# Y turned one step behind its gate, beside the sums of g, with the key search taken into the last attention steps (hgrn2 attention and a balanced expert layer)

## Chip, cores and metric

The kernel runs on one core of one Trainium2 chip. The metric is the device time of an execution in microseconds (us), lower is better. An execution that is profiled also leaves a trace, whose span is a little shorter than its own time.

## What is computed

First a recurrent attention: for each of 4 batches and 8 heads, over 768 positions with 48 dimensions, a 48x48 state is faded and added to. Then x, its output as 3072 tokens of 384, goes through a layer of 8 experts. Tokens are given to experts greedily, in the order of all logits, and each expert takes at most 384.

```python
f = 1 / (1 + np.exp(-f_logit))
for t in range(S):
    state = f[:, :, t, :, None] * state + einsum('bhd,bhe->bhde', k[:, :, t], v[:, :, t])
    y[:, :, t] = einsum('bhd,bhde->bhe', q[:, :, t], state)
x = y.transpose(0, 2, 1, 3).reshape(B * S, H * D)
logits = x @ w_gate                        # N x 8
for idx in argsort(-logits.flatten()):     # token, expert in falling order
    if assigned[tok] < 0 and counts[e] < N // E: assigned[tok] = e
for e in range(E):
    out[assigned == e] = relu(x[assigned == e] @ w1[e]) @ w2[e]
```

## The kernel before, in words

**Attention.** The 3072 positions are cut into 24 chunks of 128 (number i = 4c + b: chunk c of batch b). A chunk passes through some thirty small functions, its stages: `load_f`, `load_k`, `load_q`, `load_v` ask SP's queue for the inputs; `decays` (L166, L167, ScalarE) makes g, the logarithm of the decay; `cumulated` (L171, TensorE, bank L) sums g along the chunk; `clipped` (L176, VectorE) makes `dl` from it; `powers` and `scaled` (L187) make scaled q and k; `lengths` (L199) sums g over half chunks, `spanned` and `recorded` (L213, GpSimd) keep these; `turn_q`, `turn_k` (L232) transpose q and k on TensorE into the banks T[0] and T[1], and ScalarE copies them out (L240); `products` (L253) makes the new state's k-v products, except in the last four chunks; `scores` (L274) multiplies k and q into the banks A; `masked0`, `masked1` (L282, VectorE) copy them under a mask; `inner` (L304) and `outer` (L315) multiply them by v, and q by the old state, into the banks Y; `joined` adds the two Y banks (ScalarE copies one, L323, VectorE adds the other, L324) into `yT`; `gate` (L344) multiplies `yT` by the gate's weights, 16 small matmuls; `gated` copies the logits out; `turn_y` (L329) transposes `yT` by four matmuls into T[0], and `copy_y` (L334, ScalarE) takes it to `x`; `with_logits` (L351, GpSimd) adds the logits to the row, and `store` (L355) sends 128 rows to `xd` in memory through SP's queue.

**Order.** The order on every engine is written out by hand. A step runs all stages once, each for the chunk that its lag gives: the tuple `stages` (L358) lists stage and lag, so (`turn_y`, 3) works in step i + 3. Steps go from -1 to 25; steps 24 (`drain`, L365) and 25 (`finale`, L369) have lists of their own. `later(step, go, at)` hangs routing work into a step at the entry (None, at).

**Routing.** A token's key is its best logit, scaled by bounds on all logits (`bounds`, L505, in three parts at steps 20, 21, 22; it looks at the first four of six chunks of every batch) into `over`. `first_choices`, `overs`, `first_codes` prepare keys and choices. The search (`search`, L722) finds, for all experts at once, the key of the last token that still fits, in four digits of base 32. For each digit VectorE marks which keys are above each of 31 thresholds (`above`, L412), TensorE counts them by expert with 24 small matmuls (`cnt`, L735), VectorE takes `most` and `filled`, and one matmul adds the digit to `base` (L742). The first digit's marks and counts (`first_counts`, L545) are made during the drain and the finale. From `base` follow `code`, `kind` and each token's place (`positions`, L793), a sort by matmuls (`numbers`, L824; `sort`, L832, token matmuls L846) of the first expert's two token blocks (`found0`, `tok0`), whose rows GpSimd fetches by indirect DMA (`fetch`, L717); then the full sort, the token list, gathers of logits for tokens that are left over (L886), and fetches for experts 1 to 4.

**Experts.** `ffn` (L643) transposes the fetched rows (`Xe`, L653; copied to `xeT` by ScalarE, L656), multiplies by w1 (L664, relu into `hT`, L668), then by w2 (L678), and scatters the rows to the output (L684). TensorE's expert work is a list of pieces that are handed out between the matmuls of the leftover search by planned costs. `load_weights` (L551) asks SP's queue for an expert's two weight tensors; those of experts 0 and 1 are asked for in the end of the attention, between steps 24 and 25 and after step 25.

**Idle turns.** `idle_turns` (L106) puts matmuls of no use on TensorE: 5 ahead of the first L171, then 3, 12, 6 and 20 between the steps of the sort and ahead of the first Xe.

Of the kernel before, what the change touches and what calls it, by code (L numbers as in the profile page):

```python
# [25 lines left out]
def kernel(  # L26
# [76 lines left out]
    def idle_turns(n, tag=None):  # L103
        nothing = ps("nothing", tag) if tag else T[0]
        for _ in range(n):
            nc.tensor.matmul(out=nothing[:, 0:3 * 128], lhsT=ones16[:], rhs=idle[:], start=True,  # L106
                             stop=True)
# [120 lines left out]
    def turn_of(nm, src):  # L228
        def turn(G):
            G[nm + "_ps"] = t = T[nm == "kT"]  # L230
            for hp in range(HP):
                nc.tensor.transpose(  # L232
                    out=t[:, 128 * hp:128 * hp + 128],
                    in_=G[src][:, 2 * hp:2 * hp + 2, :].rearrange("t h d -> t (h d)"),
                    identity=ident[:])
# [84 lines left out]
    def joined(G):  # L320
        G["yT"] = yT = work.tile([128, HP, 128], FP32, name="yT", tag="yT")
        flat = yT[:].rearrange("p a t -> p (a t)")
        nc.scalar.copy(out=flat, in_=G["Y"][1][:])  # L323
        nc.vector.tensor_tensor(out=flat, in0=G["Y"][0][:], in1=flat, op=ALU.add)  # L324

    def turn_y(G):
        G["X"] = X = T[0]
# [10 lines left out]
    def gate(G):  # L338
        G["lg"] = r = (part_of(G, HP * DH)[:, 0:E] if G["i"] + 3 >= len(chunks)
                        else lengthy[:, D:D + E])  # L340
        for hp in range(HP):
            for j in range(2):
                half = slice(HC * j, HC * j + HC)
                nc.tensor.matmul(out=r[half, :], lhsT=G["yT"][:, hp, half], rhs=wg_rows[:, hp, :],  # L344
                                 start=(hp == 0), stop=(hp == HP - 1))
# [7 lines left out]
    def store(G):  # L353
        row = S * G["b"] + C * G["c"]
        nc.sync.dma_start(out=xd[row:row + C, :], in_=G["x"][:])  # L355

    chunks = [{"b": b, "c": c, "i": c * B + b} for c in range(NCH) for b in range(B)]
    stages = ((clamp, -1), (masked0, 2), (joined, 3), (turn_q, 1), (copy_q, 1), (turn_k, 1),  # L358
              (copy_k, 1), (cumulated, 0), (clipped, 0), (masked1, 2), (decays, -1), (load_f, -4),
              (load_v, -3), (lengths, 0), (products, 1), (gate, 3), (gated, 3), (turn_y, 3),  # L360
              (turned, 1), (powers, 0), (copy_y, 3), (scaled, 0), (load_k, -3), (load_q, -3),
              (spanned, 0), (next_state, 1), (faded, 0), (kept_part, 0), (recorded, 0), (None, 0),
              (with_logits, 3), (scores, 1), (inner, 2), (outer, 2), (store, 3))
    begun = tuple(x for x in stages if x[1] >= 0) + tuple(x for x in stages if x[1] < 0)
    drain = ((masked0, 2), (masked1, 2), (turn_q, 1), (joined, 3), (copy_q, 1), (turn_k, 1),  # L365
             (copy_k, 1), (turned, 1), (gate, 3), (gated, 3), (scores, 1), (None, 0), (turn_y, 3), (copy_y, 3),
             (inner, 2), (outer, 2), (masked0, 1), (masked1, 1), (None, 1), (with_logits, 3),
             (store, 3))
    finale = ((joined, 3), (inner, 2), (outer, 2), (None, 0), (gate, 3), (gated, 3), (turn_y, 3),  # L369
              (None, 1), (joined, 2), (copy_y, 3), (None, 2), (gate, 2), (gated, 2), (None, 3),  # L370
              (turn_y, 2), (copy_y, 2), (with_logits, 3), (store, 3), (with_logits, 2),
              (store, 2), (None, 4))
# [114 lines left out]
    def first_choices(b0, b1, c0, c1):  # L487
        nb, n = b1 - b0, c1 - c0
        lg, bst = columns(logits, b0, b1, c0, c1), columns(best, b0, b1, c0, c1)
# [43 lines left out]
    def first_counts(b0, b1, c0, c1, part):  # L533
# [5 lines left out]
        if "r" not in counts:  # L539
            counts["r"] = ps("cnt", "Y")  # L540
# [10 lines left out]
    def load_weights(e, pool, slot, parts=(0, 1), behind=None):  # L551
        for part in parts:
            shape, src = (([128, DC, F], moe_w1), ([128, FC, D], moe_w2))[part]
            w = pool.tile(shape, FP32, name=f"w{part + 1}", tag=f"w{part + 1}_{slot}", bufs=1)
            if behind is not None:
                nc.scalar.copy(out=w[0:1, 0, 0:1], in_=behind)
# [9 lines left out]
    for i in range(3):  # L566
        later(LAST - 3 + i, lambda: next(ranged))
    END = NCH - 1
    later(LAST, lambda: overs(0, B, 0, SEEN))
    later(LAST + 1, lambda: first_choices(0, B, SEEN, END))  # L570
    later(LAST + 1, lambda: overs(0, B, SEEN, END))
    later(LAST + 1, lambda: first_choices(0, 2, END, NCH), 1)
    later(LAST + 1, lambda: overs(0, 2, END, NCH), 1)
    later(LAST + 2, lambda: first_counts(0, B, 0, END, 0))
    later(LAST + 2, lambda: first_counts(0, B, 0, END, 1), 1)
    later(LAST + 2, lambda: first_counts(0, 2, END, NCH, 0), 2)
    later(LAST + 2, lambda: first_counts(0, 2, END, NCH, 1), 3)

    def last_choices():
        first_choices(2, B, END, NCH)  # L580
        overs(2, B, END, NCH)
        first_counts(2, B, END, NCH, 0)
        first_counts(2, B, END, NCH, 1)
# [3 lines left out]
    later(LAST + 2, last_choices, 4)  # L587
# [10 lines left out]
    later(0, lambda: idle_turns(5))  # L598
    with tc.manual_schedule(engines=FIXED):
# [6 lines left out]
        attention(-1, LAST + 2)  # L606
        load_weights(0, early, 0)
        attention(LAST + 2, ALL)
        load_weights(1, early, 1)
# [4 lines left out]
    def fast():  # L614
# [28 lines left out]
        def ffn(e, first_block, n, ahead=None):  # L643
# [5 lines left out]
            def turn(i):  # L649
                def go():  # L650
# [5 lines left out]
                    nc.scalar.copy(out=xT[:, :, 128 * i:128 * i + 128],  # L656
# [64 lines left out]

        def search(over, choice, n):  # L722

            base = bank("base", "b")
            for d in range(DIGITS):
                r = counts["r"]
                if d:
                    above = rt([n, TH], f"above{n}", FP16)
                    stt(above[:], last_of(over, TH), base[:, 0:1], mid_of(steps[d][:], n),
                        ALU.subtract, ALU.is_ge)  # L730
# [705 lines left out]
```

## Time and profile before

| what | us |
|---|---|
| three runs | 441.04, 441.70, 442.91 (median 441.7) |
| the profiled execution, its own time | 453.18 |
| its span in the trace | 451.3 |
| attention steps 3 to 23 | 20.7 to 135.0 |
| drain and finale, to the second digit's marks | 135.0 to 145.7 |
| digits two to four | 145.7 to 153.1 |
| places, sort, first fetches, to the first H | 153.1 to 166.9 |
| experts | 166.9 to 451.3 |

The profiled execution is longer than the three runs, so a sum of its rows is compared with its own time. In the rows that follow, the first number is a start in us from the span's start, the second the duration of one; then engine, line, operation, output<-input with partitions and elements, and the number of like instructions behind one another. What stands in brackets is the idle time of that engine ahead of the instruction, and what ended it. Matmul durations overlap, so what one costs is read from start to start. In the row of slices, each digit is the share of one fortieth of the span in tenths (9 is 90% or more); PEclk is TensorE's granted clock, in tenths of full speed. The busiest engine is TensorE:

```profile
PE 422.2 (94%) x4551; PEld 302.7 (67%) x4551; DVE 180.4 (40%) x612; ACT 161.1 (36%) x371; POOL 108.9 (24%) x230
```

(PE is TensorE, PEld its weight loads, DVE VectorE, ACT ScalarE, POOL GpSimd, SP SyncE.) TensorE's clock in the trace is half at 11.39 to 14.81, at 144.51 to 158.17 and at 178.65 to 188.89 us, and full elsewhere from 4.57 to 444.9.

### The profile page before, as it was taken

Reading aid. Unit: us, or ns where it says so; the run is one execution under the profiler, and the core shown is the slowest. Engines: PE = TensorE matmul, PEld = TensorE weight load, DVE = VectorE, ACT = ScalarE, POOL = GpSimd, SP = SyncE. Lnnn points to the kernel's source line nnn. Section 1 sums busy time; section 2 is a strip of 40 time slices with the busy share of each in tenths; the row PEclk is TensorE's granted clock in tenths of the full one; section 3 lists DMA queues with packets and bytes.
Section 4 is the critical chain, followed back from the end, with each engine's and each line's share of the span. In section 5 each row is a group of like instructions: output and inputs, shape, how many; then the busy total and the mean of one; then the engine's idle time right before and its main releaser. Section 6 shows DMA issues by size and latency. Waiting matters only on the chain.

```text
span 451.3 us, 10936 instructions
## 1 busy us (share of the span) xinstructions
PE 422.2 (94%) x4551; PEld 302.7 (67%) x4551; DVE 180.4 (40%) x612; ACT 161.1 (36%) x371; POOL 108.9 (24%) x230
## 2 busy tenths in 40 slices
PE   6999999999997686799999999999999999999992
PEld 3687888877776464568685858688887556556551
DVE  5688888888887631076665661000000000000000
ACT  4687777777763001122131212132332212212200
POOL 5344444444431067010100105011113203101010
PEclk9899999999999599699999999999999999999997
DMA  9899998999936927415344003049942201100000
GB/s 156 149 173 191 190 178 181 201 194 190 185 90 222 385 63 236 135 71 181 134 164 152 17 19 108 19 158 298 302 153 71 73 17 38 50 19 35 0 28 30
DMA packets 119146, 59.30 MB, mean 131 GB/s; under 512 B 102320, under 2 KB 113712, under 8 KB 119088
## 3 DMA queue, kind: packets, MB, share of 16 engines
q1 hardware_dynamic: 115824, 48.96, 43.6%
q0 software_dynamic: 3264, 9.56, 6.7%
q8 instruction: 37, 0.61, 0.5%
q14 instruction: 21, 0.17, 0.1%
HBM read 48.91 MB, written 9.54 MB: 129 GB/s over the span
## 4 chain that ended last, share of the span: by engine, by line
PE 74%; issue 13%; DVE 3%; another core or an unknown queue 2%; POOL 2%; SPq 1%; DMA 1%; ACT 1%; POOLq 0%; ACTq 0%; DVEq 0%
PE H L664 22%; PE O L678 21%; PE T L232 5%; PE A L274 4%; PE Y L304 3%; PE L L171 3%; PE T L329 3%; PE L L344 2%; PE small L253 2%; PE Y L315 2%; PE nothing L106 2%; PE small L199 1%; PE Xe L653 1%; POOL out_dram L684 1%
## 5 line engine op out<-in xcount | busy, mean ns | idle before, releaser
L664 PE MATMUL H<-xeT,w 128*128 128x256 f32 (+2 forms) x624 | 134.9, 373 | 8.1 <-ACT hT L668 7.3
L678 PE MATMUL O<-w,hT 128*128 128x384 f32 x384 | 132.6, 490 | 0.0
L664 PEld LDWEIGHTS H<-xeT,w 128*128 128x128 f32 x624 | 100.9, 194 | 36.6 <-ACT hT L668 8.4
L678 PEld LDWEIGHTS O<-w,hT 128*128 128x128 f32 x384 | 69.9, 190 | 39.2 <-issue 0.2
L684 POOL DMA_INDIRECT out_dram<-o,tok x24 | 23.3, 970 | 222.6 <-ACT o L683 217.2
L668 ACT ACTIVATE hT<-H 128x256 f32<-128x256 f32 (+2 forms) x104 | 38.0, 367 | 101.2 <-PE H L664 87.8
L683 ACT COPY o<-O 128x384 f32<-128x384 f32 x24 | 11.5, 478 | 74.5 <-PE O L678 73.0
L282 DVE COPY_PREDICATED am<-mask,A 128x512 f32<-128x512 int32 x48 | 34.5, 724 | 0.6 <-POOL spans L213 0.4
L656 ACT COPY xeT<-Xe 128x384 f32<-128x384 f32 x24 | 11.4, 478 | 60.4 <-PE Xe L653 60.4
L717 POOL DMA_INDIRECT xe<-xd,tok x24 | 23.1, 963 | 23.5 <-DVE numb L405 16.5
L274 PE MATMUL A<-qT,kT 48*64 48x128 f32 (+1 forms) x768 | 22.7, 255 | 0.1
L171 PE MATMUL L<-g,wcum 128*128 128x384 f32 x48 | 20.1, 501 | 1.8 <-ACT g L167 1.3
L274 PEld LDWEIGHTS A<-qT,kT 48*64 48x64 f32 x768 | 19.1, 136 | 3.9 <-issue 3.2
L324 DVE TENSOR_TENSOR yT<-Y,yT 128x512 f32<-128x512 f32 x23 | 15.9, 690 | 11.2 <-ACT yT L323 11.2
L409 DVE TENSOR_SCALAR full_r<-cnt,there 128x32 f32<-128x32 f32 x24 | 6.0, 251 | 34.8 <-PE cnt L777 34.8
L304 PE MATMUL Y<-am,v 64*64 64x128 f32 (+1 forms) x368 | 19.7, 244 | 0.0
L157 POOL COPY w<-v 64x256 f32<-64x256 f32 x48 | 18.9, 394 | 2.5
L304 PE MATMUL Y<-am,w 64*64 64x128 f32 (+1 forms) x368 | 19.3, 244 | 0.0
L209 POOL TENSOR_TENSOR gl<-span,spans 128x4 f32<-128x4 f32 x20 | 5.0, 250 | 55.5 <-PE A L274 39.8
L176 DVE TENSOR_SCALAR dl<-L 128x384 f32<-128x384 f32 x24 | 13.4, 557 | 12.2 <-PE L L171 12.0
L323 ACT COPY yT<-Y 128x512 f32<-128x512 f32 x23 | 13.5, 587 | 13.2 <-PE Y L315 11.0
L304 PEld LDWEIGHTS Y<-am,v 64*64 64x64 f32 x368 | 17.8, 134 | 0.2 <-issue 0.2
(220 smaller groups left out, 537.8 us busy)
## 6 DMA issues: line engine op xcount, KB each, us to landing
w<-in_moe_w_dram SPq DMA_DIRECT2D x16, 1536.0 KB, 7.2
xd<-x SPq DMA_DIRECT2D x24, 196.0 KB, 3.6
f<-in_f_logit_dram SPq DMA_DIRECT2D x24, 192.0 KB, 4.5
k<-in_k_dram SPq DMA_DIRECT2D x24, 192.0 KB, 5.0
q<-in_q_dram SPq DMA_DIRECT2D x24, 192.0 KB, 4.7
v<-in_v_dram SPq DMA_DIRECT2D x24, 192.0 KB, 4.8
xe<-xd,tok POOLq DMA_INDIRECT x24
out_dram<-o,tok POOLq DMA_INDIRECT x24
```

The lines of the kernel that those rows point to most:

```text
L157: nc.gpsimd.tensor_copy(out=w[HC * z:HC * z + HC], in_=G["v"][HC - HC * z:C - HC * z, H // 2:H])
L171: nc.tensor.matmul(out=G["Lv"], lhsT=wcum[:], rhs=g_bufs[G["i"] % NB][:, :, 0:DH], start=True, stop=True)
L232: nc.tensor.transpose(out=t[:, 128 * hp:128 * hp + 128], in_=G[src][:, 2 * hp:2 * hp + 2, :].rearrange("t h d -> t (h d)"), identity=ident[:])
L274: nc.tensor.matmul(out=A[par][to, 128 * hp + first * j:128 * hp + 128], lhsT=G["kT"][rows, hp, HC * j:HC * j + HC], rhs=G["qT"][rows, hp, ...
L282: nc.vector.copy_predicated(am[:, par].rearrange("s (a b) t -> s a b t", b=2), mask[:].unsqueeze(2).to_broadcast((128, 2, 2, 128)), A[par] ...
L304: nc.tensor.matmul(out=G["Y"][r0][DP * r:DP * r + DP, 128 * blk + first:128 * blk + 128], lhsT=v, rhs=G["am"][rows, h % 2, h // 2, first:128],
L324: nc.vector.tensor_tensor(out=flat, in0=G["Y"][0][:], in1=flat, op=ALU.add)
L664: nc.tensor.matmul(out=L["H"][:, 0:w], lhsT=slots[e][0][:, d, 128 * ft:128 * ft + 128], rhs=xT[:, d, 0:w], start=(d == 0), stop=(d == DC - 1))
L668: nc.scalar.activation(out=hT[:, ft, 0:w], in_=L["H"][:, 0:w], func=AF.Relu)
L678: nc.tensor.matmul(out=L["O"][:, 0:D], lhsT=hT[:, ft, 128 * i:128 * i + 128], rhs=slots[e][1][:, ft, :], start=(ft == 0), stop=(ft == FC - 1))
L684: nc.gpsimd.indirect_dma_start(out=outs[next(tiles)][:, :], out_offset=bass.IndirectOffsetOnAxis(ap=token(e, first_block + i), axis=0), in ...
L717: nc.gpsimd.indirect_dma_start(out=t[:], out_offset=None, in_=xd[:, :], in_offset=bass.IndirectOffsetOnAxis(ap=token(e, i), axis=0))
```

## The change

- `turn_y`, `copy_y`, `with_logits` and `store` get lag 4 instead of 3, and `turn_y` stands right behind `cumulated` instead of behind `gate`. `yT` gets a third buffer.
- The routing extras of a step stand behind `masked0`, not near the end of the step. The three parts of `bounds` come one step earlier.
- `joined` is split into `taken` (ScalarE) and `added` (VectorE). For the last chunk both Y banks are copied out at once, and its gate is summed from both parts (32 matmuls instead of 16); the sum is added up later, in a digit of the search.
- The search moves into the attention block. `turn_y`, `copy_y`, `with_logits`, `store` of chunks 21, 22 and 23 run in digits two, three and four, between marks and counts; marks are made in two halves of 12 tiles. The last chunk's best logit and choice are read from the gate's bank directly; `gated` and the late sum run in digit two, the last codes in digit three. The last three stores go through ScalarE's DMA queue.
- The weights of experts 0 and 1 are asked for only once GpSimd has copied an element of the last chunk's `y0` (one of its two Y copies) into each.
- Idle turns: 9 instead of 5 ahead of the first L171, 2 more ahead of each pair of q and k transposes of chunk 0, 3 at the end of the search (they stood ahead of the places), 20 instead of 6 behind the first sort, 3 instead of 20 ahead of the first Xe.
- The full sort reads a copy of `blk` that GpSimd makes behind the first two fetches. One of the first expert's two `xeT` copies goes to VectorE, and eight of its pieces stand ahead of two small matmuls of the leftover search.

The core of the diff:

```diff
+    def taken0(G):
+        G["y0"] = y0 = kept([128, HP, 128], FP32, "y0")
+        nc.vector.tensor_copy(out=y0[:].rearrange("p a t -> p (a t)"), in_=G["Y"][0][:])
+
+    def added0(G):
+        nc.vector.tensor_tensor(out=G["yT"][:], in0=G["y0"][:], in1=G["yT"][:], op=ALU.add)
...
-        G["X"] = X = T[0]
+        G["X"] = X = lengthy if G["i"] + B == len(chunks) else T[0]
...
+        ys = [G[nm] for nm in ("yT", "y0") if nm in G]
+        for y, hp in ((y, hp) for y in ys for hp in range(HP)):
...
+        queue = nc.scalar if G["i"] + 3 >= len(chunks) else nc.sync
+        queue.dma_start(out=xd[row:row + C, :], in_=G["x"][:])
...
-    stages = ((clamp, -1), (masked0, 2), (joined, 3), (turn_q, 1), (copy_q, 1), (turn_k, 1),
-              (copy_k, 1), (cumulated, 0), (clipped, 0), (masked1, 2), (decays, -1), (load_f, -4),
-              (load_v, -3), (lengths, 0), (products, 1), (gate, 3), (gated, 3), (turn_y, 3),
-              (turned, 1), (powers, 0), (copy_y, 3), (scaled, 0), (load_k, -3), (load_q, -3),
-              (spanned, 0), (next_state, 1), (faded, 0), (kept_part, 0), (recorded, 0), (None, 0),
-              (with_logits, 3), (scores, 1), (inner, 2), (outer, 2), (store, 3))
+    stages = ((clamp, -1), (masked0, 2), (None, 0), (joined, 3), (turn_q, 1), (copy_q, 1),
+              (turn_k, 1), (copy_k, 1), (cumulated, 0), (clipped, 0), (masked1, 2), (turn_y, 4),
+              (decays, -1), (load_f, -4), (load_v, -3), (lengths, 0), (products, 1), (gate, 3),
+              (gated, 3), (turned, 1), (powers, 0), (copy_y, 4), (scaled, 0), (load_k, -3),
+              (load_q, -3), (spanned, 0), (next_state, 1), (faded, 0), (kept_part, 0),
+              (recorded, 0), (with_logits, 4), (scores, 1), (inner, 2), (outer, 2), (store, 4))
...
+    finale = ((taken, 3), (inner, 2), (added, 3), (outer, 2), (gate, 3), (taken, 2), (taken0, 2),
+              (gate, 2), (gated, 3), (None, 1), (None, 2), (None, 3))
...
+    def search(over, choice, n):
+        base = A[1][:, 128:129]
+        for d in range(DIGITS):
+            r = counts["r"]
+            if d:
+                above, r = rt([n, TH], f"above{n}", FP16), Y[d % 2]
+                for h in range(2):
+                    part = slice(n * h // 2, n * (h + 1) // 2)
+                    stt(above[:, part], last_of(over[:, part], TH), base,
+                        mid_of(steps[d][:], n // 2), ALU.subtract, ALU.is_ge)
+                if d == 1:
+                    gated(chunks[-1])
+                    added0(chunks[-1])
+                elif d == 2:
+                    last_codes()
+                for go in (turn_y, copy_y, with_logits, store):
+                    go(chunks[d - DIGITS])
...
-        attention(-1, LAST + 2)
-        load_weights(0, early, 0)
-        attention(LAST + 2, ALL)
-        load_weights(1, early, 1)
+        attention(-1, ALL)
+        for e in range(2):
+            load_weights(e, early, e, behind=chunks[-1]["y0"][0:1, 0, 0:1])
+        base = search(over0[:], choice0, NT)
...
-            idle_turns(6, "A")
+            idle_turns(20, "A")
...
-            r, _ = sort(line, numbers(blk, value[:], blocks[:], NT, NQ), NT, NQ, 12, in_line)
+            blk_all = rt([NT], "blk_all", FP16, 1)
+            nc.gpsimd.tensor_copy(out=blk_all[:], in_=blk[:])
+            r, _ = sort(line, numbers(blk_all, value[:], blocks[:], NT, NQ), NT, NQ, 12, in_line)
...
-            idle_turns(20, "A")
+            idle_turns(3, "A")
```

## The prediction

> **What bounds the kernel now.** I read the page's slices first, then the stretches, then TensorE's timeline inside one step, then the timelines of the end. The slices:
>
> ```profile
> PEclk9899999999999599699999999999999999999997
> DMA  9899998999936927415344003049942201100000
> ```
>
> For a third of the span (the attention) TensorE runs at full clock and the DMA engines are nearly as full; then both fall. The stretches (microseconds; busy time of each engine, granted clock, DMA share, GB/s):
>
> ```profile
> core 0: us, PE busy (x) PEld busy (x) DVE busy (x) ACT busy (x) POOL busy (x), PEclk, DMA share, GB/s
> ...
> 20.70:135.00 114.30, 113.41 (x2722) 90.01 (x2722) 94.70 (x242) 84.66 (x186) 47.24 (x147) 1.00 0.90 178
> 135.00:145.70 10.70, 9.20 (x225) 7.79 (x221) 7.42 (x28) 4.24 (x8) 1.68 (x8) 0.94 0.55 197
> 145.70:153.10 7.40, 2.93 (x76) 2.56 (x77) 3.85 (x10) 0.00 (x0) 0.00 (x0) 0.50 1.05 389
> 153.10:166.90 13.80, 12.57 (x100) 7.63 (x99) 8.09 (x32) 0.86 (x2) 4.97 (x5) 0.82 0.55 186
> 166.90:189.10 22.20, 14.80 (x49) 11.35 (x50) 1.97 (x8) 2.85 (x9) 10.38 (x11) 0.77 0.47 147
> ```
>
> In the first, TensorE is busy 113.4 of 114.3 us: there time goes only where TensorE does less or its matmuls sit closer. The next three are a serial chain: drain, key search, sort, first tokens. TensorE in one attention step:
>
> ```profile
> 80.65 0.81 PE L171 MATMUL L<-g,wcum 128*128 128x384 f32 x2
> 81.39 0.43 PE L199 MATMUL small<-g,ind 128*32 128x128 f32 x8
> 81.75 0.56 PE L253 MATMUL small<-v,kg 128*48 128x48 f32 x16
> 82.14 0.61 PE L344 MATMUL L<-wg_rows,yT 128*64 128x8 f32 x16
> 82.68 0.66 PE L329 MATMUL T<-ident,yT 128*128 128x128 f32 x4
> 83.27 0.90 PE L274 MATMUL A<-qT,kT 48*64 48x128 f32 x32
> ```
>
> Read starts against starts: L171 costs .74, L199 .36, L253 .39, L344 .54, L329 .59. L171 and L329 use the full array; each stands ahead of (L329 also behind) smaller tiles.
>
> **Own time.** The profiled execution took 453.18 (span 451.3), against a median of 441.7. Its last stretch above holds two waits that I take to be its own:
>
> ```profile
> 177.67 0.38 ACT L668 ACTIVATE hT<-H 128x256 f32<-128x256 f32 x1 [5.03 <-remote]
> 183.29 0.94 ACT L668 ACTIVATE hT<-H 128x256 f32<-128x256 f32 x3 [5.24 <-remote]
> ```
>
> Expert 0's 48 up matmuls took 22.27 us there, against 48 x 0.214 = 10.27 at the later pitch: 12.0 too many, and 453.18 - 12.0 = 441.2, the median. So the sum is set against 453.18 with that stall, and against 441.7 without it.
>
> **Part by part. Steps.** Y's transposes (L329) go behind L171, with a lag of 4 steps instead of 3. Between two full-array groups L171 keeps its own pitch, .65 instead of .74, and L329 .53 instead of .59; L344 then meets the scores at the same gap as L329 did (.13). Saved .148 a step. It holds in steps 4 to 19: 16 x .148 = 2.4. Step 3 loses its L329 (.59), because chunk 0 turns a step later. Steps 20 to 23 have other waits: this one (three alike, .29 each) stood in 21 to 23, since no products lie between L199 and the gate:
>
> ```profile
> 120.50 0.64 PE L344 MATMUL L<-wg_rows,yT 128*64 128x8 f32 x16 [0.29 <-DVE dl L176]
> ```
>
> L329 behind L171 covers it. So step 23 gives .29 + .15 = .44. Step 22 took 5.79, .31 more than step 23's 5.48, for extras queued on VectorE ahead of `dl`; these move up a step: .44 + .31 = .75. They now burden step 21: 1.4 us between the first mask and `yT`'s add hold up `dl` and the second mask, and eat all of its .44 but .2 by my list of starts. Step 20 gets a bounds matmul between L329 and the kT copy, +.07. Together -1.3 (.07 - .2 - .75 - .44). Attention: -(2.4 + .6 + 1.3) = -4.3. The turn of chunk 20 is thereby moved to the end and priced there.
>
> The cover for this is DMA: a load must land before its step. Slack (landing to use) of k is 1.5 us at chunk 5, 2.3 at 10, 3.2 at 15, 4.4 at 20; of q about .3 at chunk 3 and 1.1 to 1.8 at 4 to 9. Steps shortened by .148 bring uses forward by 1.3 by step 12, just inside q's slack; one store less ahead of the early loads gives about .25 back. Without the cover, steps keep DMA's pace (about 5.25 us) and 2 of the 4.3 go.
>
> **Startup.** Nine idle turns instead of five before the first L171 (+.78), two more ahead of each pair of q/k transposes, and a half-clock stretch at 11.4 to 14.8 that they may fill (-1.1). But this path ends on a transfer, not on TensorE:
>
> ```profile
> 20.10 0.56 DVE L187 TENSOR_TENSOR qg<-q,eq 128x384 f32<-128x384 f32 x1 [0.39 <-DMA q<-in_q_dram]
> ```
>
> q of chunk 2 landed at 20.01 and step 3 follows from it. Both ends -.3 and +.3; I take 0.
>
> **Drain and first digit.** From the drain's first transpose (134.97) to the first `above` (below, 145.66) are 10.69 us. TensorE's work ahead of it loses two turns (of 21 and 22, .59 each) and 23's (.6), gains 20's, and the second part of the last gate (.54). My list of starts: scores +1.80, inner of 22 +2.5, gate 21 +3.7, inner of 23 +4.15, its outer to +5.46, gate 22 to +6.0; the two halves of the last Y are copied at once on ACT (.59) and DVE (.69) instead of one after the other, gate 23 +6.33 to +7.4; maxima, choice, `over`, half of `above` on DVE +8.34; two count matmuls, `most`, `filled`, `base`: +9.3. Gain 1.4.
>
> **Digits.**
>
> ```profile
> 145.66 1.00 DVE L412 SCALAR_TENSOR_TENSOR above<-over,base,step 128x744 f16<-128x744 f32 x1 [0.28 <-PE base L742]
> 147.55 0.15 DVE L415 TENSOR_REDUCE most<-cnt 31x1 f32<-31x8 f32 x1 [0.89 <-PE cnt L735]
> 147.74 0.14 DVE L409 TENSOR_SCALAR filled<-most 31x1 f16<-31x1 f32 x1
> 148.14 1.00 DVE L412 SCALAR_TENSOR_TENSOR above<-over,base,step 128x744 f16<-128x744 f32 x1 [0.25 <-PE base L742]
> ```
>
> 2.48 a digit: 1.00 `above`, .89 behind counts, the rest small. Two halves of `above` cost 1.14, but 12 of 24 counts go beside the second half. Turns, copies, and stores of 21 to 23 fill TensorE and ACT; on DVE `gated` and `added0` (.87) queue ahead of `most` in digit 1 and the codes in digit 2. Gains .02, .14, .19: .35. Had the turns no cover, 3 x .59 would come back.
>
> **To the tokens.** From the codes to `found0` 6.11, unchanged. Then:
>
> ```profile
> 160.60 1.19 POOL L717 DMA_INDIRECT xe<-xd,tok  x1 [16.53 <-DVE numb L405]
> ```
>
> The first fetch stood 1.03 behind its token (159.57), behind DVE's full `numb`. With the POOL copy `blk_all`, `numb` waits for both fetches: behind that wait stand the full sort, the token list, the six gathers and the fetches of experts 1 to 4, about 2.3 us later; the leftover search that needs them starts on TensorE 2.9 us after its inputs, so 0 for the rest. So the early fetch saves 1.03 at the issue, but Xe stands on TensorE behind the full sort. Before, that ended at 162.1, 20 idle turns (3.43) ran to 165.3, and Xe (165.28) came out of them, a microsecond behind the second landing (164.30). Now, counted from `found0`: token .36, two fetches 1.19 + .31 + .94, copy of blk .15, `numb` 1.06, 24 matmuls 1.51, 3 turns .49 = 6.01, less .06 of overlap = 5.95; the landings come at about 5.0. So the queueing behind `numb` is swapped for one behind the fetches. I count .12 for 5.95 against 6.07 (ends -.5 and +.5) and .1 for the second `xeT` copy on DVE beside ACT's (Xe to H 1.5 against 1.6): .2. End in all: 1.4 + .35 + .2 = 1.95.
>
> The weights of experts 0 and 1 wait for `y0` on POOL; behind these on POOL are `with_logits` of 21 to 23, on SP nothing but the weights. Before, they were issued 139.5 to 145.8 and took until 160.7, 15 us after the last issue. Now I put the last landing at +24.5 of the drain, H at +30: covered by 5; without cover the excess counts one for one.
>
> Stores of the last three go on ACT's queue. Row: the last two stores on SP, behind weights, landed 8.2 and 7.9 us after issue, median of all 3.6. The Trainium skill, "DMA: Bandwidth & Descriptors", section "Queues, rings and completion order", has the engines take turns between queue rows by packet, so another row would not stand behind SP's weights: the last store lands at +19.5 and the fetch (+22.9) waits for nothing. By the row, 8.2, it lands at +24 and costs 1.1. The same page's section "Issuing engines are not separate DMA queues" speaks against: the transfers share the same 16 engines, and only issue time is saved. I take the first (0), since the last store is 0.2 MB against the weights' 6, and keep 1.1 for the range: no run here shows ACT's row.
>
> **The clock.** The skill, "TensorE: Matmul & The Clock Gate", section "Part 1: The HAM clock gate", halves the clock after an idle window of about 3.4 us. Row: it fell at 144.51 and stayed half for 13.65 us, though no gap on TensorE exceeded 1.09 us. So matmuls of 8 columns with short gaps seem not to hold it. By the rule the changed kernel, with 3 idle turns ahead of Xe instead of 20 (14 moved earlier), keeps full clock into H; by the row it can fall there. The row decides that it can happen; that 17 of 20 are only moved is why I give it little.
>
> **Rivals.**
> - DMA binds the steps (.13): gain 4, 437.5 to 438.5. For: DMA share .90; against: slack grows along the attention.
> - The end's gain is lost (.10): fetch behind the store, VectorE's order in digit 1: 437.4 to 439.
> - Slower (.06): the clock is halved at the start of expert 0. A half-clock stretch like that of 178.65 to 188.89 (10.24 us) costs 5.1; two cost 10.2: 445.6. It decides above 12.6 us of half clock (half of it eats 6.3). For: the row of 144.51; against: H is dense.
> - More (.09): the turns between digits keep the clock full through the search, or the startup gains: 430 to 433.
>
> **The number.** 4.3 + 0 + 1.95 = 6.3. From 441.7: 435.4; against the profiled execution, 446.9 with the stall, 434.9 without. Main case (.62) 433 to 438. Expert work beyond is taken unchanged: 8 pieces set earlier, 0. The range is 431.5 to 439.5. Half a per cent, 2.2 us, is about what can be told from no change: faster .86 (main, more, most of two rivals), same .09, slower .05.
>
> **What would show it.** L171 and L329 starting .65 and .53 apart; steps of 5.34; no wait on `dl`; first `above` at +9.3; first fetch right behind its token. Wrong if qT waits for loads from step 8 on, if weights or stores land after Xe is ready, or if PEclk shows half during H.

## The result, and the profile after

The changed kernel takes 439.49 us (median of 22 executions, 437.92 to 443.87) against 441.5 of the kernel before (22 executions beside it): a ratio of 0.9961, 95% interval 0.9944 to 0.9979. So it is faster by 2.0 us, where 6.3 were forecast, and it lies at the upper edge of the range (439.5): less than a third of the forecast came. Two later comparisons of the unaltered kernel give 0.9956 (0.9941 to 0.9972) and 0.9951 (0.9935 to 0.9966).

In two of the six comparisons, called "on a chip of 452" from here on, the kernel before takes 452 us in every execution, because TensorE's completions in expert 0 reach ScalarE late there, so each ratio holds only against the kernel before in the same comparison. The profiled execution of before (453.18) looks like these.

The profiled execution after took 441.33 (span 439.5). The clock's slices on its page:

```profile
PEclk9999999999999588999999999999999999999997
```

The three low slices in a row (5, 8, 8) are two dips: the clock is half at 141.19 to 154.84, in the search, and again at 161.67 to 168.50, from Xe into expert 0. By stretches, cut at the same events as before (step 3, drain, second digit's marks, `code`, first H):

```profile
core 0: us, PE busy (x) PEld busy (x) DVE busy (x) ACT busy (x) POOL busy (x), PEclk, DMA share, GB/s
20.73:132.36 111.63, 110.64 (x2723) 90.64 (x2718) 96.57 (x244) 80.87 (x184) 46.23 (x145) 1.00 0.91 181
132.36:141.74 9.38, 8.29 (x234) 7.37 (x231) 7.23 (x25) 3.27 (x7) 2.59 (x13) 0.97 0.28 71
141.74:148.82 7.08, 5.81 (x88) 4.58 (x89) 5.51 (x19) 1.43 (x3) 0.59 (x1) 0.50 1.02 394
148.82:164.55 15.73, 12.98 (x94) 7.96 (x94) 7.61 (x25) 0.48 (x1) 4.12 (x5) 0.72 0.75 273
164.55:168.50 3.95, 3.95 (x9) 3.17 (x10) 0.15 (x3) 0.38 (x1) 2.97 (x4) 0.50 0.08 3
```

The first three are shorter than before (114.26, 10.69, 7.44). The fourth is longer: 15.73 against 13.79. In the fifth, 3.95 us of expert 0 run at half clock. TensorE in a step after:

```profile
68.00 0.81 PE L171 MATMUL L<-g,wcum 128*128 128x384 f32 x2
68.65 0.60 PE L344 MATMUL T<-ident,yT 128*128 128x128 f32 x4
69.18 0.43 PE L199 MATMUL small<-g,ind 128*32 128x128 f32 x8
...
69.93 0.60 PE L361 MATMUL L<-wg_rows,yT 128*64 128x8 f32 x16
70.46 0.90 PE L276 MATMUL A<-qT,kT 48*64 48x128 f32 x32
```

(The changed file's L344 is before's L329, L361 is L344, L276 is L274.) Sums .65, Y's transposes .53, scores .53 behind the gate: the step is 5.33. But some steps wait for q; in VectorE's timeline:

```profile
77.24 0.56 DVE L187 TENSOR_TENSOR qg<-q,eq 128x384 f32<-128x384 f32 x1 [0.69 <-DMA q<-in_q_dram]
...
82.93 0.56 DVE L187 TENSOR_TENSOR qg<-q,eq 128x384 f32<-128x384 f32 x1 [0.67 <-DMA q<-in_q_dram]
```

And the end. The first expert's token is VectorE's `tok`; before, then after:

```profile
159.40 0.17 DVE L409 TENSOR_SCALAR tok<-found 128x2 int32<-128x2 f32 x1
```

```profile
155.13 0.17 DVE L426 TENSOR_SCALAR tok<-found 128x2 int32<-128x2 f32 x1
```

GpSimd after, then TensorE before and after:

```profile
156.32 1.18 POOL L769 DMA_INDIRECT xe<-xd,tok  x1 [12.73 <-DMA w<-in_moe_w_dram]
157.81 0.95 POOL L769 DMA_INDIRECT xe<-xd,tok  x1 [0.31 <-issue]
158.76 0.21 POOL L900 COPY blk_all<-blk 128x24 f16<-128x24 f16 x1
```

```profile
160.62 1.51 PE L846 MATMUL tokens<-numb,in_line 128*128 128x30 f16 x24 [0.46 <-DVE numb L405]
161.96 3.43 PE L106 MATMUL nothing<-idle,ones 128*128 128x384 f16 x20
...
165.28 0.85 PE L653 MATMUL Xe<-ident,xe 128*128 128x128 f32 x6
```

```profile
154.76 3.43 PE L106 MATMUL nothing<-idle,ones 128*128 128x384 f16 x20
160.16 1.51 PE L874 MATMUL tokens<-numb,in_line 128*128 128x30 f16 x24 [1.97 <-DVE numb L422]
161.50 1.02 PE L106 MATMUL nothing<-idle,ones 128*128 128x384 f16 x3
162.31 1.49 PE L704 MATMUL Xe<-ident,xe 128*128 128x128 f32 x6
164.55 2.05 PE L716 MATMUL H<-xeT,w 128*128 128x256 f32 x4 [0.75 <-issue]
```

The token ends at 155.30, the fetch starts at 156.32: 1.02 later, as before (159.57 and 160.60: 1.03), though no `numb` ran on VectorE. TensorE stands still for 1.97 us until the full `numb` is made, which waits for the copy behind both fetches. At 161.67 the clock falls to half until 168.5, so Xe takes 1.49 instead of .85.

Where the 6.3 went, from the two profiles (`found0` is counted from the start of VectorE's `found`): drain 2.61 earlier (4.3 forecast); first `above` another 1.31 (1.4); digits .36 (.35); `code` to `found0` 0 (0); `found0` to first H 9.61 instead of 7.67, so -1.94 (+.2). H stands 2.33 earlier. Then expert 0 loses about 2.0 in the half-clock stretch (3.95 x 1/2): .3 remains in this execution, 441.33 against 441.5. Executions with a granted clock of .98 or more (14 of 22) lie at 437.9 to 440.6, those under it at 440.5 to 443.9. The median is among the first, and all three profiles of the changed kernel are of the others.

### The profile page after: what moved, and what is told of

Its sections match the earlier page's. It is cut to its first block, busy times and chain, and to the rows that moved or that the text cites. A ratio compares the mean times of both kernels' runs of the same rounds, so it can differ in the third digit from the quotient of the medians.

```text
span 439.5 us, 11007 instructions
## 1 busy us (share of the span) xinstructions
PE 419.9 (96%) x4576; PEld 305.1 (69%) x4576; DVE 184.1 (42%) x621; ACT 157.5 (36%) x370; POOL 109.7 (25%) x235
## 4 chain that ended last, share of the span: by engine, by line
PE 69%; issue 15%; DMA 6%; DVE 3%; POOL 3%; ACT 2%; SPq 0%; POOLq 0%; DVEq 0%
PE H L716 23%; PE O L730 21%; PE T L234 4%; DMA w<-in_moe_w_dram 4%; PE A L276 3%; PE L L171 3%; PE Y L306 3%; PE L L361 2%; PE T L344 2%; PE small L255 2%; PE Xe L704 2%; PE Y L317 1%; POOL out_dram L736 1%; DMA q<-in_q_dram 1%; PE small L199 1%
## 5 line engine op out<-in xcount | busy, mean ns | idle before, releaser
L716 PE MATMUL H<-xeT,w 128*128 128x256 f32 (+2 forms) x624 | 132.7, 370 | 0.8 <-issue 0.8
L276 PE MATMUL A<-qT,kT 48*64 48x128 f32 (+1 forms) x768 | 22.3, 251 | 0.4 <-ACT kT L242 0.3
L171 PE MATMUL L<-g,wcum 128*128 128x384 f32 x48 | 19.7, 491 | 1.0 <-ACT g L167 1.0
L306 PE MATMUL Y<-am,v 64*64 64x64 f32 (+1 forms) x368 | 19.8, 243 | 0.0
L276 PEld LDWEIGHTS A<-qT,kT 48*64 48x64 f32 x768 | 18.7, 133 | 1.4 <-ACT kT L242 0.5
L234 PE MATMUL T<-ident,qg 128*128 128x128 f32 x96 | 15.8, 285 | 2.2 <-DVE qg L187 2.0
L344 PEld LDWEIGHTS T<-ident,yT 128*128 128x128 f32 x92 | 11.6, 150 | 8.8 <-ACT qT L242 5.6
L209 POOL TENSOR_TENSOR gl<-span,spans 128x4 f32<-128x4 f32 x20 | 3.9, 196 | 54.2 <-DVE span L206 33.2
L306 PEld LDWEIGHTS Y<-am,w 64*64 64x64 f32 x368 | 17.3, 134 | 0.0
```

The source lines that it names most:

```text
L171: nc.tensor.matmul(out=G["Lv"], lhsT=wcum[:], rhs=g_bufs[G["i"] % NB][:, :, 0:DH], start=True, stop=True)
L234: nc.tensor.transpose(out=t[:, 128 * hp:128 * hp + 128], in_=G[src][:, 2 * hp:2 * hp + 2, :].rearrange("t h d -> t (h d)"), identity=ident[:])
L276: nc.tensor.matmul(out=A[par][to, 128 * hp + first * j:128 * hp + 128], lhsT=G["kT"][rows, hp, HC * j:HC * j + HC], rhs=G["qT"][rows, hp, ...
L306: nc.tensor.matmul(out=G["Y"][r0][DP * r:DP * r + DP, 128 * blk + first:128 * blk + 128], lhsT=v, rhs=G["am"][rows, h % 2, h // 2, first:128],
L344: nc.tensor.transpose(out=X[:, 128 * hp:128 * hp + 128], in_=G["yT"][:, hp, :], identity=ident[:])
L716: nc.tensor.matmul(out=L["H"][:, 0:w], lhsT=slots[e][0][:, d, 128 * ft:128 * ft + 128], rhs=xT[:, d, 0:w], start=(d == 0), stop=(d == DC - 1))
```

## The experiments

Theory: the steps gain as forecast, and the gain is lost in three places: loads that come late, the full sort's wait behind GpSimd with the clock that falls in it, and weights that hold the first rows. Rivals: the new order of the engines simply saves less; the early full sort is all there is; the start costs it. There were 18 runs.

**The turn alone (twice).** The kernel before with

```diff
-              (copy_k, 1), (cumulated, 0), (clipped, 0), (masked1, 2), (decays, -1), (load_f, -4),
+              (copy_k, 1), (cumulated, 0), (clipped, 0), (masked1, 2), (turn_y, 4), (decays, -1), (load_f, -4),
```

and lag 4 for `copy_y`, `with_logits`, `store`; chunk 20's turn stands in the drain, and `yT` has three buffers.

> The kernel before with one part of the change alone: Y's transposes, their copy and store get lag 4, the transposes stand behind the sums of g; chunk 20's are done in the drain. If the attention's gain is cut by the pace of the loads, the drain starts at 132.0 to 132.8 us (134.97 before, 132.36 with the whole change) with steps of 5.33 only where q lands early, and the time is about 439.5 (2.6 off the attention, 0.6 paid back for chunk 20 in the drain). If my sum of 4.3 was right for this part and something else of the change spoiled it, the drain starts at 130.7 and the time is about 437.8.

> Once more the kernel before with the later turn of Y alone, as the first run of it fell on a chip where the kernel before takes 452. There the drain started at 130.61 instead of 134.97 and the first H at 164.34 instead of 166.88. So I expect 2.5 to 3.5 below the kernel before, 438.0 to 439.0: no less than the whole change gives. If it gives under 1.5, the rest of the change is worth more than I say.

Ratios 0.9934 (0.9906 to 0.9962) and 0.9904 (0.9873 to 0.9934), both on chips of 452. In the profiles the drain starts at 130.61 and 130.27 (134.97 and 134.64 before), with steps of 5.33 and no wait for q after step 4. First H: 164.34 and 163.98. So this part gives the forecast 4.3 by itself, and H is as early as in the whole change (164.55, 165.29 and 163.24 in its three profiles). It is so although 3.0 us lie between Xe and H here, where completions come late (1.6 in the first profile of before). Xe itself stands at 161.32 and 160.97, against 162.31, 163.05 and 161.28. From step 3 to the drain the turn alone takes 110.02 and 110.03, and no version with the extras behind `masked0` takes less than 110.4. The first expectation's second case held (130.7). The second expectation, 2.5 to 3.5, was too low for a chip of 452 (5.0); on a chip of 441.5 the turn alone was not timed.

**Fewer loads, and the control.** Both kernels leave out the loads of v for chunks 7 to 23 and use old v again:

```diff
+            if nm == "v" and G["i"] >= NV:
+                return
             t0 = C * G["c"]
```

> The changed kernel with the v loads of chunks 7 to 23 left out (old v are used again), so that 3.3 MB less have to come in during the attention. If the loads' pace binds, the waits of qg for q in steps 13 to 19 go, all these steps take 5.33, the drain starts near 131.4 instead of 132.36, and the time is about 1 us lower than the changed kernel's (438.5). If the steps are bound by the engines' order, the drain stays at 132.3 and the time at 439.5 within 0.5.

> Control: the kernel before with the same v loads left out. Its steps of 5.48 do not wait for loads from step 6 on, so by both theories the drain stays at 135.0 within 0.3 and the time at 441.5 within 0.5. If it gains as much as the changed kernel does from the same cut, the loads cost both kernels alike and don't explain the missing gain.

The ratio is 0.9816 (0.9784 to 0.9847), on a chip of 452, so the profile has to tell. The changed kernel's waits for q are gone and its steps 6 to 18 are all 5.32 to 5.36; from step 3 to the drain 110.42 (111.63, 112.10, 111.02 in the unaltered one's three profiles). The drain itself stood at 132.21 for another reason: step 3 began at 21.79 instead of 20.7. The control stays: 0.9995 (0.9978 to 1.0012), 114.27 from step 3 to the drain. So, against 110.42, late loads cost the changed kernel 0.6 to 1.7 in those executions, and the kernel before nothing. This run alone does not decide that: no version that began step 3 so late (21.4 and more) waited for q, with all its loads in. It is VectorE's waits for q in the rows above that name the loads.

**Fill the gap (twice).**

```diff
-            idle_turns(20, "A")
+            idle_turns(32, "A")
```

> The changed kernel with 32 instead of 20 idle turns behind the first sort, which fill the 1.97 us in which TensorE waits for the full numb. If the half-clock window at 161.7 comes from that gap, it goes, Xe takes 0.85 instead of 1.49 and the first H matmuls their full pitch; the time falls to about 438.0 and the runs lie closer together. If the gap does not decide the clock, the time stays 439.5 within 0.5 and some runs still show a clock of 0.97 to 0.976.

> Once more the changed kernel with 32 instead of 20 idle turns behind the first sort and nothing else, as the first run of it fell on a chip where the kernel before takes 452. If TensorE's gap ahead of the full sort halves the clock, the window at 161.8 to 168.7 is gone, and the time is about 438.3, 1.3 below the changed kernel; if the early full sort itself was what the version without the copy gained, 439.6.

The second run is on a chip of 441.5: 438.52, 0.9934 (0.9917 to 0.9951), 1.2 under the unaltered kernel's 439.76 on a chip of the same kind; the intervals of the two ratios (control 0.9941 to 0.9972) overlap a little, so the profile decides. (The first: 0.9861, 0.9827 to 0.9894, on a chip of 452.) TensorE's timeline in the second:

```profile
154.32 5.36 PE L106 MATMUL nothing<-idle,ones 128*128 128x384 f16 x32
159.71 1.51 PE L874 MATMUL tokens<-numb,in_line 128*128 128x30 f16 x24
...
161.55 0.82 PE L704 MATMUL Xe<-ident,xe 128*128 128x128 f32 x6
```

No gap; Xe takes .82, the clock stays full from 153.16 to 433.05. All six executions show .978 or more. `found0` to Xe is 7.05, hardly changed (7.37, 7.50 and 7.08 in the unaltered kernel's three profiles), so it is the gap that lets the clock fall, and the clock that costs. The other profiles agree: in all 7 with the gap (1.6 to 2.0 us) the clock falls at 160.4 to 162.0; in the 8 profiles of changed versions without it, it falls nowhere between 155.1 and 180. In two of the 7 (fewer loads, and early weights with the copy, below) the dip is 3.4 us long and over before H.

**Control, extras, copy, warm-up (one chip).** The unaltered kernel; the extras moved back to the end of the step (`(None, 0)` there again, bounds at steps 20 to 22); the copy of blk taken out,

```diff
-            nc.gpsimd.tensor_copy(out=blk_all[:], in_=blk[:])
-            r, _ = sort(line, numbers(blk_all, value[:], blocks[:], NT, NQ), NT, NQ, 12, in_line)
+            r, _ = sort(line, numbers(blk, value[:], blocks[:], NT, NQ), NT, NQ, 12, in_line)
```

and an indirect fetch of nothing used in the third digit:

```diff
+                if d == 2:
+                    nc.gpsimd.indirect_dma_start(
+                        out=warm[:], out_offset=None, in_=moe_w2[0],
+                        in_offset=bass.IndirectOffsetOnAxis(ap=zero[:, 0:1], axis=0))
```

> The changed kernel again, unaltered, as the control for the three others on the same chip, and as a second profile of it. If the late loads of steps 13 to 19 are systematic, the drain starts at 132.3 to 133.8 us again and q waits show; if they were the luck of one execution, it starts near 131.0 to 131.5. Against the kernel before I expect either 0.9961 as in the first comparison or, where the kernel before shows the long wait for the second hidden tile of expert 0 (as on the chip of the first four runs, 452), about 0.985.

> The changed kernel with the routing extras put back to the end of the step and the three bounds parts back to steps 20 to 22. If the extras behind the first mask are what made steps 20 and 21 take 5.73 and 6.04 instead of 5.34, these two come down to 5.33 and 5.2, the drain starts about 1.0 earlier than in the unaltered changed kernel and the time falls by about 0.7. If those steps were late for loads, nothing changes within 0.3.

> The changed kernel without GpSimd's copy of blk: the full numb runs on VectorE right behind the first token, as before. If the copy frees the first fetch, the fetch moves from 1.02 to over 1.0 later than now. If, as the two traces suggest (1.03 before, 1.02 after), VectorE's numb never held the fetch, the fetch starts at 1.02 again, the full sort comes 2.3 us earlier, TensorE has no gap ahead of it, and Xe waits for the rows alone: Xe about 0.5 to 1.0 earlier, and the time falls by 0.5 to 2 (the latter if the clock then stays full).

> The changed kernel with one more indirect fetch on GpSimd (128 rows of the weights into a tile that nobody reads) in the third digit, long before the first token. If the 1.02 us between the token and the first fetch are the cost of the first indirect transfer after a long pause, they fall to about 0.3, as for the gathers behind, and Xe comes 0.7 earlier. If they belong to the waits that the first fetch has (ten semaphores), they stay at 1.0.

Control 439.76. Extras back 440.2, 0.9961 (0.9944 to 0.9978): no gain, where .7 was expected. Its steps 19 to 23 sum to 26.56, the control's to 26.78, so my two slow steps were exchanged for others. (This edit also put the idle turns of step 0 back behind the first sums: step 3 began at 20.17, .7 earlier, and steps 12 to 16 took 1.3 more than 5 x 5.33, with waits for q.) Warm-up 441.51, 0.9994: a loss. GpSimd in it:

```profile
154.98 0.96 POOL L775 DMA_INDIRECT xe<-xd,tok  x1 [12.52 <-DMA w<-in_moe_w_dram]
```

The token ended at 154.11: .87 later, against an expected .3. So `numb` is not the reason, and an earlier use takes only .15 off; GpSimd's waits end at 154.23 and .75 pass before the instruction starts. The rows landed 6.6 us behind their issue (4.9 in the changed kernel), together with the last weight (161.73). That weight took 20.6 us from its issue instead of 18.4; I put this down to the additional fetch, which no run shows.

Without the copy 438.04, 0.9926 (0.9910 to 0.9941; the control 0.9941 to 0.9972). TensorE:

```profile
160.95 1.01 PE L704 MATMUL Xe<-ident,xe 128*128 128x128 f32 x6 [1.11 <-issue]
162.81 1.53 PE L716 MATMUL H<-xeT,w 128*128 128x256 f32 x6 [0.85 <-ACT xeT L708]
```

`found0` to Xe falls from 7.4 to 6.19, the fetch still starts 1.03 behind its token (156.15), and the clock stays full. The rows in between:

```profile
154.95 0.17 DVE L426 TENSOR_SCALAR tok<-found 128x2 int32<-128x2 f32 x1
156.15 1.19 POOL L769 DMA_INDIRECT xe<-xd,tok  x1 [12.67 <-DVE numb L422]
```

Now Xe waits for the rows, which landed at 160.86, half a microsecond behind the last weight (160.36).

**Weights, start (one chip).** Without the copy, and the weights asked for behind the drain, with no wait for `y0`; without the copy, and the start without the added turns (5 instead of 9, and none ahead of chunk 0's transposes); all of these.

```diff
-        attention(-1, ALL)
-        for e in range(2):
-            load_weights(e, early, e, behind=chunks[-1]["y0"][0:1, 0, 0:1])
+        attention(-1, LAST + 2)
+        for e in range(2):
+            load_weights(e, early, e)
+        attention(LAST + 2, ALL)
```

```diff
-    later(0, lambda: idle_turns(9))
+    later(0, lambda: idle_turns(5))
```

> The changed kernel without GpSimd's copy of blk, and with the weights of experts 0 and 1 asked for right behind the drain's store, without a wait for y0. In four profiles the first expert's rows landed 0.4 to 0.5 us behind the last weight (160.69 then 161.18, 161.15 then 161.59, 160.02 then 160.42, 160.36 then 160.86), 4.7 us behind their issue. If the weights hold the rows up, weights that are asked for 4 us earlier land by 157, the rows 3 to 3.5 us behind their issue at 159.5, Xe starts about 1.3 us earlier than in the version without the copy alone (160.95 with a start of the first transposes at 10.8), and the time falls from 438.0 to about 436.8. If 4.7 is simply what the rows take, nothing changes. A loss would show as stores that land later, behind which the first fetch waits.

> The changed kernel without the copy of blk, and with the start as before: 5 idle turns ahead of the first sums, none ahead of the q and k transposes of chunk 0. The first transposes begin at 9.8 to 10.8 us with the change's start, 8.9 to 9.6 with the old one, but step 3 waits for q of chunk 2. If the new start costs time, the drain starts 0.4 to 0.8 earlier and the time falls to about 437.5; if q's landing covers it, 438.0 within 0.3; if the clock's half at 11 to 15 us returns and counts, up to 439.

> The changed kernel without the copy of blk, with the early weights and with the old start: both effects add, 436.2 to 436.8, or 438.0 if neither counts. This is the version that should beat both kernels.

Weights: 437.39 (436.8 expected), 0.9911 (0.9888 to 0.9934), by its time alone not told apart from the version without the copy. They landed by 156.05, the rows 3.24 and 3.04 behind their issue, and Xe starts at 159.48, 4.92 behind `found0` (6.19 with the late weights); the second block's transposes still wait for their rows:

```profile
160.52 0.55 PE L705 MATMUL Xe<-ident,xe 128*128 128x128 f32 x3 [0.55 <-DMA xe<-xd,tok]
```

Start: 438.36, 0.9938 (0.9916 to 0.9959), no gain. One sentence ahead of the prediction is wrong: in the kernel before, the five turns run behind the first sums (at 6.94, sums at 5.77), not ahead of them; only the change puts them ahead, and this version left five there. So it undoes the start in part only, and the start proper was not tried alone. Both: 437.34 (436.2 to 436.8 expected), 0.9901 (0.9884 to 0.9918), the lowest time of all, though not told apart from the early weights alone; against the changed kernel's 0.9961 its interval lies wholly below.

**What was open (two comparisons).** The kernel before again; the early weights with the copy kept; the version without the copy and with early weights, with k and q asked for a step earlier (four buffers each), twice; the changed kernel a third time.

> The kernel before, for a second profile of it. Where its time is 441.5, the two waits of 5 us for the second hidden tiles of expert 0 should be missing, and expert 0's 48 up matmuls should take 10.3 to 10.7 us; where it is 452, they are there. So it tells whether the 12.0 us that I took off as a stall of the profiled execution are that. It also shows whether the kernel before ever waits for late loads in steps 6 to 19 (I expect none: 114.3 from step 3 to the drain, as in its two profiles so far).

> The changed kernel with the early weights alone; GpSimd's copy of blk stays. The rows should land 3 to 3.3 us behind their issue, but Xe stands behind the full sort, which waits for the copy: Xe does not move, TensorE's gap of 2 us stays, the half-clock window at about 162 stays in most executions, and the time is 439.6 within 0.5. If the weights were the main loss, it falls to 438.9 or below.

> The version without the copy of blk and with the early weights, and k and q asked for one step earlier with a fourth buffer each. If the late loads in some executions come from too short a lead, the waits of qg for q go in every execution and the runs lie closer together, at 436.5 to 437.2 (437.39 without the lead). If the transfers' rate sets the pace, a longer lead helps only until it is used up, and the time stays 437.4; the two loads more at the start can cost up to 0.8, since they come ahead of f and v of the next chunks.

> Once more the version without the copy of blk, with early weights and with the longer lead of k and q; its first run fell on a chip where the kernel before takes 452, and q then landed 3.5 to 8 us ahead of its use in every step. If the chip is of the other kind (before 441.5), I expect 436.5 to 437.3; if of this kind, 442.4 again.

> The changed kernel, unaltered, beside it. On a chip where the kernel before takes 441.5 it gives 439.6 and the version beside it is 2.5 to 3 faster. On a chip where the kernel before takes 452, it gives about 444 to 445: then the change gains some 7 us there, because less of the long wait in expert 0 is left, and its gain depends on the chip.

The first three fell on a chip of 452. ScalarE's timeline there, in the kernel before:

```profile
178.70 0.38 ACT L668 ACTIVATE hT<-H 128x256 f32<-128x256 f32 x1 [5.71 <-remote]
```

The first of the two waits of the first profile again; the second, 3.83 us, follows at 182.91. All 18 executions took 450.2 to 452.9: so what I took for the first profile's own stall comes in every execution of such a comparison. Early weights with the copy: 443.76, 0.9841 (0.9796 to 0.9886) there, no comparison with 439.6. Its profile agrees with the theory: `found0` to Xe stays 7.50, the gap stays 1.99, the clock is half at 160.66 to 164.07. So in this profile early weights bring nothing while the copy stands. The longer lead: 442.42, 0.9787 (0.9758 to 0.9815), and on a chip of 441.2 438.42, 0.9937 (0.9918 to 0.9956): q lands 3.4 us or more ahead in every step, yet the time is not under 437.4, and step 3 begins at 21.6. The lead removes the waits, not the late start. The changed kernel beside it: 439.19, .8 more, where 2.5 to 3 were expected.

One profile each, in us (late loads: what the stretch from step 3 to the drain takes over 110.4), and the timed median:

| kernel | step 3 at | drain at | late loads | `found0` to H | H at | time, ratio |
|---|---|---|---|---|---|---|
| before | 20.7 | 134.97 | - | 7.67 | 166.88 | 441.5 |
| changed (first) | 20.73 | 132.36 | 1.2 | 9.61 | 164.55 | 439.49, .9961 |
| changed (control) | 20.88 | 132.97 | 1.7 | 9.74 | 165.29 | 439.76, .9956 |
| changed (third) | 20.68 | 131.70 | .6 | 9.04 | 163.24 | 439.19, .9951 |
| gap filled | 21.58 | 131.99 | 0 | 8.62 | 163.12 | 438.52, .9934 |
| no copy | 21.77 | 132.24 | .1 | 8.05 | 162.81 | 438.04, .9926 |
| no copy, early weights | 21.43 | 131.88 | 0 | 7.36 | 161.92 | 437.39, .9911 |
| the same, five turns | 21.73 | 132.20 | .1 | 7.32 | 162.02 | 437.34, .9901 |

## Why the prediction was right and wrong

- **Steps.** Right: .148 a step forecast, .15 measured (5.48 to 5.33), no wait on `dl` worth naming. Steps 19 to 21 took 5.44, 5.73, 5.65 in undisturbed executions; I had 5.33, 5.55, 5.39, so .55 is missing (the extras: put back, these steps took 5.33, 5.33 and 5.17), and .14 is gained in 22 and 23 (4.97 each against 5.04). From step 3 to the drain 3.84 were gained (114.26 to 110.42), 4.3 forecast.
- **DMA as the cover.** I wrote that it just holds. It mostly did not: of the profiles with the changed steps and all loads, 6 of the 7 that began step 3 before 21.0 had late loads, by .4 to 2.6 in all; none of the 5 that began at 21.4 or later had them by more than .1. An early start is eaten by the loads, and a late one hides them. So rival one came in beside the main case. The turn alone had no late loads in two profiles with step 3 at 20.2 and 20.6; why not is open.
- **Startup.** "Both ends -.3 and +.3; I take 0" was too narrow. Step 3 began at 20.7 to 20.9, or, where TensorE's clock came up at 6 us or later instead of 4.6 to 4.9, at 21.4 to 21.9: up to 1.2 lost, since 22 idle turns then run partly at half clock ahead of the first sums (7.64 instead of 5.77). The kernel before began step 3 at 20.4 to 20.7 in its profiles, also where its clock came up at 5.9. The sum missed that idle turns ahead of real work cost their own time, at whichever clock is granted.
- **Drain, digits, code.** Right: +9.38 (9.3 forecast), digits .36 (.35), 6.12 (6.11). The stores on ACT's queue landed 6.0 to 6.7 us behind their issue; the last at +22.3 of the drain, between my estimates of 19.5 and 24. It held up nothing. The Trainium skill's "DMA: Bandwidth & Descriptors", section "Queues, rings and completion order", has the engines take turns between queue rows; the last store (154.62) did land ahead of weights that were issued before it on SP's row (160.69).
- **To the tokens: the step that failed.** Forecast 5.95 from `found0` to Xe and 1.5 to H; measured 7.37 and 2.24 in the first profile (6.07 and 1.60 before). "So the early fetch saves 1.03 at the issue" is false: `numb` on VectorE never held it. About .9 pass on GpSimd between the end of its waits and the start of the fetch, with `numb` beside it or not, so that the fetch starts 1.02 behind its token; what these .9 are is open. The sum of 5.95 has no term for them, and as it put the full sort behind both fetches, they came in full: 1.02 of the 1.42 that are missing. Some .3 more are the last turns at half clock (sort to Xe 2.15, with the gap filled 1.84). The sum also held that the rows land at about 5.0 behind `found0`; they took 6.2 and 6.7. And it did not set TensorE's turns against the sort: the 20 turns end at +3.3, by the sum's own terms the sort cannot start ahead of +4.0, and it started at +5.2. The gap between was there to be seen. (The working's second landing before, 164.30, stands in no row; the last packets of the two fetches end at 164.74, so Xe came half a microsecond behind them.)
- **The weights.** "I put the last landing at +24.5 of the drain" was +28.3 (160.69), and the cover that mattered was not H's need of the weights but the rows that share the transfers: 4.9 and 3.9 us to land instead of 3.2 and 3.0 with early weights.
- **The clock.** I gave .06 to a half-clock stretch at H. It is there in all three profiles of the changed kernel, 6.8 us long, and costs 2.0 in H and .6 from Xe to H; 5.1 for 10.2 us was the price I had set, so the price was right and the chance was not. (From the first H to the end of the span, 274.8 to 275.8 us pass in the five profiles with the dip in H, and 273.0 to 273.9 in the six without it, all outside the chips of 452.) The Trainium skill's "TensorE: Matmul & The Clock Gate", section "Part 1: The HAM clock gate", asks for an idle window of about 3.4 us; here 1.97 us without work, followed by 1.5 us of thin matmuls (30 columns), were enough, and filling the gap ended it.

So the mechanism forecast for the attention was right, and the one forecast for the first fetch was wrong. Three of the rivals (late loads, the end's gain lost, half clock at expert 0) came in together, each in part, where I had weighed them as alternatives. Of the missing 4.3, 1.7 lie ahead of the drain (2.6 gained there as a mean of the three profiles, 4.3 forecast: .5 in the steps, the rest late loads) and up to 2.1 between `found0` and H. The 2.0 of H's clock fall on executions that have the dip (8 of 22 show a clock under .98), not on the median; no execution like the median was profiled, so the split of its 4.3 is an estimate from the others, and about .5 has no place. The versions without the copy and with early weights come to 437.4; 435.4 was not reached by any.

## What to carry to other kernels

A wait that is added to let an early transfer go first must be checked twice: that the transfer was really held by what is moved behind it (an unchanged 1.02 us told that it was not), and what the engine that now idles does to its clock. A gain in a stream's pace is bounded by the loads' lead at its start, so look at slack step by step over several executions, not in one.

## What was not expected of the hardware

Without late completions, expert 0's 48 up matmuls take 10.7 us, and ScalarE starts on a hidden tile .04 behind its last matmul (167.06 and 167.10 in the version without the copy). On the chips of 452, hidden tiles waited 4 to 8 us in all versions: in the second profile of before the third tile of H ended at 172.07, and ScalarE started on it at 178.70. The next weights (3 MB) and GpSimd's fetches move in that stretch, but they do so in the other comparisons too. The changed versions lost less there: 0.9841 and 0.9861 against 0.995. Why is open, and it need not be the chip: the record names chip 4 for the first comparison of 452 and again, an hour later, for one of 441.2.
